# Attention stage of a fused fp32 kernel: value products of a head pair in three runs instead of four, in two PSUM banks

## Chip, cores and metric

The kernel runs on one core of a Trainium2 chip. The metric is the device time of one execution in microseconds (us): before the change 931.25 us, the median of 3 runs (930.16 to 931.75).

## What is computed

The program is an attention with pooled queries, followed by two feed-forward blocks. The change touches the attention alone:

```python
B, H, S, D = 4, 8, 1152, 64
q_pool = q.reshape(B, H, S // 2, 2, D).mean(axis=3)     # 576 queries a head
scores = (1 / sqrt(D)) * q_pool @ k.transpose(0, 1, 3, 2)
scores -= max(scores, axis=-1)
attn = exp(scores);  attn /= sum(attn, axis=-1) + 1e-9
out = attn @ v                                          # then the two blocks
```

All of it is fp32. The 32 heads are worked on as 16 pairs; after them the two blocks (matmuls with weights that the attention stage prepares on the side) take the rest of the time.

## The kernel before

**Tiles.** A pair P has nine score tiles of 128 query rows by 1152 keys: four for each head, and one (the fifth) that holds the 64 last rows of both heads. I number them 0 to 8 within the pair. Tiles alternate between two PSUM buffers of three banks each (`SC`, shown as `sc`). Two more banks, `TX` and `TY` (shown as `tx` and `ty`), serve everything else.

**One score tile** passes four stations: `scores` on TensorE (six matmuls of 384 keys, L303), `smax` on VectorE (the negated row maximum, `m`, L324), `sexp` on ScalarE (the exponential with the row sum, L336), and then a transposition, since the value product needs the keys on the partitions. There are two ways to transpose. Tiles 0 to 3 of every pair but the first are "block-turned": VectorE turns 32 by 32 blocks into the buffer `BLK` (`turn_blocks`, L356), and 16 DMAs move the blocks to their places in the tile `E` (`move_blocks`, L365, issued once a pair by SyncE). Tiles 4 to 8 are transposed by TensorE, 128 keys at a time, into PSUM (`fill`, L389: one block into the tile's own score bank, called "o", four into `ty` and four into `tx`) and copied to the tile `M` (`take`, L400: "o" and "y" by ScalarE, "x" by VectorE).

**Value products.** `E` holds the first 256 query columns of a pair (group 0), `M` the other 320 (group 1). `pv_part` (L423) multiplies one of nine key blocks of a group, for both heads: two matmuls, which the trace records as two each, so 18 matmuls and 36 records make a group. `pv_copy` (L433) copies the finished group from PSUM to the output buffer on ScalarE; `norm2` (L469, GpSimd) multiplies it with the reciprocal row sums later.

**Order.** Engines take their instructions in the order in which they are written. The loop over s, the running number of a tile (L658), writes step s like this:

```python
gaps[s]                        # pv_copy among them
take_rest()                    # "y" copy of tile s - 1
turn_blocks, sexp(s + 1), ...  # if tile s is block-turned; else fill "o", take "o", sexp(s + 1)
mids[s]
scores(s + 2)
fill(s, "y"), fill(s, "x")     # if tile s is not block-turned
smax(s + 2)
take(s, "x")                   # as above
run_pv(s)                      # value products planned for this step
sched[s]
```

So TensorE computes scores two tiles ahead, and the value products of a step stand behind the scores of that step. `shares` (L341) says in which steps the value products of pair P run, counted from the pair's first step, as (step, number of key blocks): steps 9 to 12 are steps 0 to 3 of the next pair, the four block-turned tiles, where TensorE has nothing to transpose. `pv_copy` of a group stands in the gap of the step after its last block.

**Side work.** Two tables place other work into these steps. `PREP` names the steps (with 0, 1, 2 for gap, mid and end of a step) of the preparation of the next pair; `qd` is `q_double`, a ScalarE copy of one head's query parts (L259). `PIECES` does so for the preparation of a piece of a weight: `mag` (ScalarE, L127) and `clamp` (GpSimd, L130), then three bit operations on VectorE (L134, L138, L142), then `hi`, `lo` and a store. Its load (512 KB) stands at the end of the step before the pair; SyncE issues it behind the 16 block moves and two stores, and ahead of the loads of the next keys and queries (`kn` and `qn`, 576 KB each).

Of the kernel before, what the change touches and what calls it, by code (L numbers as in the profile page):

```python
# [26 lines left out]
NP = NB * NH // 2  # L27
# [16 lines left out]
NORM = 9  # L44

PREP1 = ((1, 0, 'kh'), (1, 0, 'qs'), (1, 0, 'qm'), (1, 2, 'qo', 0), (2, 0, 'kt', 0), (2, 2, 'kl', 0, 0), (3, 0, 'kl', 0, 1), (4, 0, 'qo', 1), (4, 2, 'kt', 1), (5, 0, 'kl', 1, 0), (5, 2, 'kl', 1, 1), (5, 2, 'lk'), (5, 2, 'lq'), (5, 2, 'qd', 0), (7, 2, 'qd', 1), (20, 1, 'lv'))
PREP = ((-1, 2, 'qs'), (0, 0, 'qm'), (0, 0, 'qo', 0), (0, 2, 'qo', 1), (1, 1, 'lk'), (1, 1, 'kh'), (2, 0, 'lq'), (2, 1, 'qd', 0), (2, 2, 'kt', 0), (3, 1, 'kt', 1), (3, 1, 'qd', 1), (4, 2, 'kl', 0, 0), (5, 0, 'kl', 0, 1), (6, 0, 'kl', 1, 0), (6, 2, 'kl', 1, 1), (20, 1, 'lv'))

PIECES = {"a": ((1, 2), ((2, 2), (2, 2), (2, 2)), (9, 2), 14, 15), "x": ((1, 2), ((2, 2), (2, 2), (2, 2)), (3, 2), 5, 7)}
LATE = 5  # L50
LATE_TICK = 14
LATE_PACE = 2
# [11 lines left out]
def attn_moe_kernel(ctx: ExitStack, tc: tile.TileContext, qT, kT, vP, muk, mur, wk, wv, wr, wth, wtr, wti, wch, ident, out):  # L64
# [94 lines left out]
    def attention(first):  # L159
# [11 lines left out]
        TX = psV.tile([128, 512], F32, tag="tx", name="tx")  # L171
        TY = psV.tile([128, 512], F32, tag="ty", name="ty")
# [48 lines left out]
        kts, vns, rss, raws, qs = {}, {}, {}, {}, {}  # L221
# [58 lines left out]
        def quick(P):  # L280
            return P > 0
# [59 lines left out]
        def shares(P):  # L341

            if P == NP - 1:
                return ((8, 9),), ((8, 9),)
            return ((9, 5), (10, 4)), ((11, 5), (12, 4))

        pvs = {}

# [62 lines left out]
        def pv_part(k, x):  # L411

            P, g = k
            w = groups[g][1]
            j = (x + 3) % KT
            if x == 0:
                pvs[k] = TX if k == (NP - 1, 0) else TY
            for h in range(2):
                e = Es[k][:, h, j]
                out = pvs[k][64 * h:64 * h + 64, :w]  # L420
                if g == 0 and quick(P):
                    out = out.rearrange("p (a q) -> p a q", a=4)
                pe.matmul(out, lhsT=vns[P][:, h, j], rhs=e, start=(x == 0), stop=(x == KT - 1))  # L423
# [66 lines left out]
        for P in range(NP):  # L490
            for g, when in sorted(enumerate(shares(P)), reverse=P == NP - 1):
                j = 0
                for o, m in when:
                    n = min(P * KT + o, NT)
                    plan.setdefault(n, []).extend(((P, g), j + x) for x in range(m))
                    j += m
                assert j == KT
                if P == NP - 1:
                    at(n, pv_copy, (P, g))
                else:  # L500
                    at_gap(n + 1, pv_copy, (P, g))
            if P == NP - 1:
                for step in (norm0, norm1, norm3):
                    at(NT - 1, step, P)
                at_mid(NT, spread, P)
                at(NT, norm2, P)
            else:
                at(P * KT + NORM, norm0, P)
                at(P * KT + NORM + 1, norm1, P)
                at_mid(P * KT + NORM + 2, norm3, P)  # L510
                at(P * KT + NORM + 2, spread, P)
                at_mid(P * KT + NORM + 4, norm2, P)
            if quick(P):
                at(P * KT + 2, move_blocks, P)

        def run_pv(s):
            for k in plan.pop(s, []):
                pv_part(*k)
# [3 lines left out]
        def prep_sched(P):  # L522
            base = (P - 1) * KT
            for o, hook, name, *args in (PREP if P > 1 else PREP1):
                if P + (name[0] == "l") < NP and (P > 1 or base + o >= 3 or name != "lv"):
# [105 lines left out]
        for P in range(1, NP):  # L631
            base = P * KT
            for kind, (i, piece) in zip("x" if P == NP - 1 else "a", pieces):
                (zm, hm), bits, (z, hz), zl, zs = PIECES[kind]
                load, mag, clamp, *cuts, hi, lo, store = conv_steps(lambda i: cp.tile([128, 1536], F32R, tag="cv", name="cv"), piece, i, engines[CLO], pool)
# [601 lines left out]
```

## Time and profile before

| | us |
|---|---|
| median of 3 runs | 931.25 (930.16 to 931.75) |
| the profiled execution | 932.49 |
| its span, first to last instruction | 930.5 |
| TensorE matmuls busy | 907.8 (98%) |
| VectorE busy | 686.7 (74%) |
| GpSimd busy | 594.2 (64%) |
| ScalarE busy | 541.9 (58%) |
| idle time of the row maxima (L324) before they start, waiting for scores | 47.8 |
| idle time of the exponentials (L336), waiting for the maximum | 56.2 |

Matmuls are pipelined and their ends are modelled in the trace, so TensorE's busy share says little; start times of consecutive instructions say more. In the rows, PE is TensorE's matmuls, PEld its weight loads, DVE VectorE, ACT ScalarE, POOL GpSimd, SPq the queue of SyncE.

### The profile page before, as it was taken

Reading aid. Unit: us, or ns where it says so; the run is one execution under the profiler, and the core shown is the slowest. Engines: PE = TensorE matmul, PEld = TensorE weight load, DVE = VectorE, ACT = ScalarE, POOL = GpSimd, SP = SyncE. Lnnn points to the kernel's source line nnn. Section 1 sums busy time; section 2 is a strip of 40 time slices with the busy share of each in tenths; the row PEclk is TensorE's granted clock in tenths of the full one; section 3 lists DMA queues with packets and bytes.
Section 4 is the critical chain, followed back from the end, with each engine's and each line's share of the span. In section 5 each row is a group of like instructions: output and inputs, shape, how many; then the busy total and the mean of one; then the engine's idle time right before and its main releaser. Section 6 shows DMA issues by size and latency. Waiting matters only on the chain.

```text
span 930.5 us, 17357 instructions
## 1 busy us (share of the span) xinstructions
PE 907.8 (98%) x6292; PEld 786.4 (85%) x6292; DVE 686.7 (74%) x965; ACT 541.9 (58%) x1133; POOL 594.2 (64%) x662
## 2 busy tenths in 40 slices
PE   8999999999999999999889999998999999999998
PEld 6677777777777777768888999998999999999998
DVE  7888888888898888872699888888347663676712
ACT  8777777777777777764645565555344343443310
POOL 7877777777788777763466565666347574674631
PEclk9999999999999999999989999999899999999999
DMA  7268886777777776669323323233206200010001
GB/s 242 86 176 227 237 225 187 218 211 207 217 213 210 209 235 186 186 183 365 137 70 112 103 86 103 86 119 124 107 1 213 82 27 27 1 51 2 26 26 51
DMA packets 58773, 129.74 MB, mean 139 GB/s; under 512 B 10752, under 2 KB 29888, under 8 KB 58688
## 3 DMA queue, kind: packets, MB, share of 16 engines
q1 hardware_dynamic: 58688, 128.64, 46.4%
q8 instruction: 49, 0.80, 0.4%
q14 instruction: 36, 0.29, 0.1%
HBM read 70.46 MB, written 22.17 MB: 100 GB/s over the span
## 4 chain that ended last, share of the span: by engine, by line
PE 83%; DVE 8%; ACT 4%; issue 3%; POOL 1%; DMA 0%; SPq 0%; ACTq 0%; DVEq 0%; POOLq 0%
PE sc L303 18%; PE ty L423 16%; PE ps L1129 12%; PE ps L834 7%; PE ps L853 7%; PE ps L1148 5%; PE ps L1075 5%; PE ty L389 4%; PE tx L389 3%; PE ps L803 2%; PE sc L389 2%; DVE a L134 1%; DVE a L138 1%; ACT e L336 1%; PE ps L1033 1%
## 5 line engine op out<-in xcount | busy, mean ns | idle before, releaser
L324 DVE TENSOR_REDUCE m<-sc 128x1 f32<-128x1152 f32 x138 | 185.8, 1346 | 48.5 <-PE sc L303 47.8
L336 ACT ACTIVATE e<-sc,m 128x1152 f32<-128x1152 f32 x144 | 176.4, 1225 | 60.8 <-DVE m L324 56.2
L303 PE MATMUL sc<-kt,q 128*128 128x384 f32 (+1 forms) x864 | 192.7, 351 | 3.1 <-ACT M L400 1.7
L303 PEld LDWEIGHTS sc<-kt,q 128*128 128x128 f32 (+1 forms) x864 | 146.7, 190 | 24.4 <-issue 13.6
L834 PE MATMUL ps<-x,a 128*128 128x288 f32 x768 | 107.3, 300 | 5.8 <-DVE xt L858 4.8
L1129 PE MATMUL ps<-b,a 128*128 128x288 f32 x816 | 111.3, 296 | 0.0
L834 PEld LDWEIGHTS ps<-x,a 128*128 128x128 f32 x768 | 105.1, 193 | 6.8 <-DVE xt L858 5.5
L1129 PEld LDWEIGHTS ps<-b,a 128*128 128x128 f32 x816 | 109.4, 188 | 0.6
L853 PE MATMUL ps<-k,b 128*128 128x288 f32 x768 | 103.8, 295 | 0.1
L853 PEld LDWEIGHTS ps<-k,b 128*128 128x128 f32 x768 | 102.1, 188 | 0.6 <-ACT h L836 0.4
L202 POOL TENSOR_TENSOR kt<-kn,kh 64x576 fp32r<-64x576 f32 (+1 forms) x64 | 87.5, 1387 | 2.4
L356 DVE STREAM_TRANSPOSE blk<-e 128x1152 f32<-128x1152 f32 x60 | 81.6, 1360 | 7.4 <-ACT e L336 7.4
L423 PE MATMUL ty<-M,vn 128*64 128x320 f32 x576 | 84.4, 438 | 0.2 <-ACT M L400 0.2
L423 PEld LDWEIGHTS ty<-M,vn 128*64 128x64 f32 x576 | 38.7, 136 | 36.3 <-issue 3.8
L469 POOL TENSOR_TENSOR xt<-xt,rb 128x576 f32<-128x576 f32 x16 | 21.9, 1371 | 73.0 <-ACT xt L433 73.0
L821 POOL TENSOR_TENSOR k<-h,k 128x288 fp32r<-128x288 f32 x64 | 56.4, 897 | 18.1 <-ACT k L820 16.1
L423 PE MATMUL ty<-E,vn 128*64 128x256 f32 x540 | 64.9, 385 | 0.0
L803 PE MATMUL ps<-x,blk 128*128 128x288 f32 x384 | 56.8, 310 | 6.9 <-ACT x L782 3.5
L803 PEld LDWEIGHTS ps<-x,blk 128*128 128x128 f32 x384 | 55.1, 201 | 8.4 <-ACT x L782 4.0
L837 DVE TENSOR_TENSOR h<-h 128x288 f32<-128x288 f32 x64 | 38.5, 606 | 27.7 <-ACT h L836 27.3
L1093 ACT ACTIVATE q<-q 128x512 f32<-128x512 f32 x18 | 11.4, 632 | 79.2 <-DVE q L1090 79.2
L783 POOL TENSOR_TENSOR x<-t,x 128x288 fp32r<-128x288 f32 x52 | 44.9, 881 | 18.0 <-ACT x L782 18.0
(147 smaller groups left out, 1751.1 us busy)
## 6 DMA issues: line engine op xcount, KB each, us to landing
E<-blk SPq DMA_DIRECT2D x240, 144.0 KB
vn<-vP SPq DMA_DIRECT2D x16, 576.0 KB
kn<-kT SPq DMA_DIRECT2D x15, 576.0 KB
qn<-qT SPq DMA_DIRECT2D x15, 576.0 KB
b<-wtk SPq DMA_DIRECT2D x9, 576.0 KB
rb<-scr SPq DMA_DIRECT2D x32, 144.0 KB
out<-xt SPq DMA_DIRECT2D x32, 144.0 KB
cv<-wk SPq DMA_DIRECT2D x8, 512.0 KB
```

What stands on the lines that cost most here:

```text
L202: engines[e].tensor_tensor(out, x, hi.bitcast(F32), ALU.subtract)
L303: r = pe.matmul(sc[0:m, c, 0:384], lhsT=x, rhs=k[:, 384 * c:384 * c + 384], start=(i == 0), stop=(i == len(ops) - 1),)
L324: r = dve.tensor_reduce(m, scs[n][:, :, 0:384], axis=AX.XY, op=ALU.max, negate=True)
L336: r = act.activation(e, sc[:, :, 0:384], AF.Exp, bias=m, scale=1.0, accum_out=rss[P][:, t:t + 1])
L356: dve.transpose(out, es_[n].rearrange("p a b -> p (a b)").rearrange("p (k m i) -> p k m i", k=KT, m=4))
L389: r = pe.transpose(ps[:, 128 * j:128 * j + 128], flat[:, 128 * k:128 * k + 128], idn)
L423: pe.matmul(out, lhsT=vns[P][:, h, j], rhs=e, start=(x == 0), stop=(x == KT - 1))
L803: pe.matmul(pss[d], lhsT=WR[k][:, w, 128 * d:128 * d + 128], rhs=x[k][:, c], start=(k == 0 and n == 0), stop=(k == 3 and n == 2))
L821: pool.tensor_tensor(q[:, 1], h, q[:, 0].bitcast(F32), ALU.subtract)
L834: pe.matmul(ps, lhsT=WK[k, f // 4][:, w, 128 * (f % 4):128 * (f % 4) + 128], rhs=x[k][:, c], start=(k == 0 and n == 0), stop=(k == 3 and n ...
L853: pe.matmul(pss[d], lhsT=WV[f][:, w, 128 * d:128 * d + 128], rhs=k2[f][:, c], start=(f == 0 and n == 0), stop=(f == 7 and n == 2))
L1129: pe.matmul(pss[d], lhsT=zs[j][z][:, 128 * d:128 * d + 128], rhs=WTK[min(j, 8)][:, w, cs], start=(m == 0 and n == 0), stop=(m == 8 and n = ...
```

## The change

Four lines change. The value products of a pair run in steps 9, 10 and 11 instead of 9 to 12: six key blocks of group 0, then three of group 0 and three of group 1, then six of group 1. Group 1 accumulates in the bank `tx` instead of `ty`; the last pair keeps its banks. The second `qd` moves from the middle of step 3 to the end of step 2. `mag` and `clamp` move from the end of step 1 to the end of step 0, and the first two bit operations from step 2 to step 1; the third stays.

```diff
-PREP = (... (3, 1, 'kt', 1), (3, 1, 'qd', 1), (4, 2, 'kl', 0, 0), ...)
+PREP = (... (3, 1, 'kt', 1), (2, 2, 'qd', 1), (4, 2, 'kl', 0, 0), ...)
-PIECES = {"a": ((1, 2), ((2, 2), (2, 2), (2, 2)), (9, 2), 14, 15), ...}
+PIECES = {"a": ((0, 2), ((1, 2), (1, 2), (2, 2)), (9, 2), 14, 15), ...}
...
-            return ((9, 5), (10, 4)), ((11, 5), (12, 4))
+            return ((9, 6), (10, 3)), ((10, 3), (11, 6))
...
             if x == 0:
-                pvs[k] = TX if k == (NP - 1, 0) else TY
+                pvs[k] = TX if g == (P < NP - 1) else TY
```

The first place is TensorE in the four block-turned steps of a pair. `sc` are score buffers, `ty` and `tx` the two other banks, `E` and `M` the transposed exponentials, `vn` the values. The tile with `kh,qc` is the fifth (tile 4), whose three kinds of matmul come three times. Before:

```order
L423 MATMUL ty<-E,vn 64x256 x10
L303 MATMUL sc_121<-kt,q_0_1_125 128x384 x6
L423 MATMUL ty<-E,vn 64x256 x8
L303 MATMUL sc_120<-kh,qc_128 128x384
L303 MATMUL sc_120<-kt,q_0_0_124 64x384
L423 MATMUL ty<-M,vn 64x320 x10
L303 MATMUL sc_121<-kt,q_0_0_124 128x384 x6
L423 MATMUL ty<-M,vn 64x320 x8
L389 MATMUL sc_120<-idn,e 128x128
```

and now:

```order
L423 MATMUL ty<-E,vn 64x256 x12
L303 MATMUL sc_121<-kt,q_0_1_125 128x384 x6
L423 MATMUL ty<-E,vn 64x256 x6
L423 MATMUL tx<-M,vn 64x320 x6
L303 MATMUL sc_120<-kh,qc_128 128x384
L303 MATMUL sc_120<-kt,q_0_0_124 64x384
L423 MATMUL tx<-M,vn 64x320 x12
L303 MATMUL sc_121<-kt,q_0_0_124 128x384 x6
L389 MATMUL sc_120<-idn,e 128x128
```

The eight matmuls of group 1 that stood behind the scores of tile 5 (the last L303 row of each piece) now stand ahead of them, and the transposition of tile 4 follows those scores directly.

The second place is ScalarE in the same steps. L336 are the exponentials of tiles 2, 3 and 4, L433 the copies of the two groups, L259 the two query copies, L127 is `mag`:

```order
-L336 ACTIVATE e,rs_140<-sc_120,m 128x1152
-L127 ACTIVATE cv<-cv 128x512
+L127 ACTIVATE cv<-cv 128x512
+L336 ACTIVATE e,rs_140<-sc_120,m 128x1152
 L433 COPY xt_69<-ty 128x4x2x32
 L336 ACTIVATE e,rs_140<-sc_121,m 128x1152
 L259 CAST q_1_0_126<-q_1_0_126 64x1152
-L336 ACTIVATE e,rs_140<-sc_120,m 128x1152
 L259 CAST q_1_1_127<-q_1_1_127 64x2x576
-L433 COPY xt_69<-ty 128x320
+L433 COPY xt_69<-tx 128x320
+L336 ACTIVATE e,rs_140<-sc_120,m 128x1152
```

`mag` goes ahead of the exponential of tile 2, and the exponential of tile 4 goes behind the second query copy and behind the copy of group 1.

The third place is VectorE. L356 are the block turns of tiles 2 and 3, L324 the row maximum of tile 4 and, in the last row, of tile 5; L134, L138 and L142 are the bit operations:

```order
 L448 STREAM_TRANSPOSE rt<-r_141 128x32
-L356 STREAM_TRANSPOSE blk<-e 128x9x4x32 x2
-L324 TENSOR_REDUCE m<-sc_121 128x1
-L134 TENSOR_SCALAR cv<-cv 128x512
-L138 SCALAR_TENSOR_TENSOR cv<-cv 128x512
+L134 TENSOR_SCALAR cv<-cv 128x512
+L138 SCALAR_TENSOR_TENSOR cv<-cv 128x512
+L356 STREAM_TRANSPOSE blk<-e 128x9x4x32 x2
+L324 TENSOR_REDUCE m<-sc_121 128x1
 L142 SCALAR_TENSOR_TENSOR cv<-cv 128x512
 L324 TENSOR_REDUCE m<-sc_120 128x1
```

Two bit operations go ahead of the two turns and of the maximum of tile 4. On GpSimd `clamp` goes ahead of the cast of the next pair's keys (L199, `kh`); SyncE's order is the same.

## Rows read from the trace of the kernel before

**Rows 1.** Part 4 of the profile's page: the chain that ended last, shares of the span.

```profile
PE 83%; DVE 8%; ACT 4%; issue 3%; POOL 1%; DMA 0%; SPq 0%; ACTq 0%; DVEq 0%; POOLq 0%
```

**Rows 2.** Timeline, TensorE, steps 2 to 4 of one pair: start, length, instruction, count.

```profile
222.25 2.91 PE L423 MATMUL ty<-M,vn 128*64 128x320 f32 x20
225.09 1.34 PE L303 MATMUL sc<-kt,q 128*128 128x384 f32 x6
226.36 2.37 PE L423 MATMUL ty<-M,vn 128*64 128x320 f32 x16
228.67 0.33 PE L389 MATMUL sc<-idn,e 128*128 128x128 f32 x1
228.75 1.29 PE L303 MATMUL sc<-kt,q 128*128 128x384 f32 x6
229.88 0.60 PE L389 MATMUL ty<-idn,e 128*128 128x128 f32 x4
```

**Rows 3.** Timeline, VectorE, block turn of tile 3, maxima of tiles 4, 5, 6, [idle before].

```profile
222.20 1.38 DVE L356 STREAM_TRANSPOSE blk<-e 128x1152 f32<-128x1152 f32 x1 [0.52 <-ACT e L336]
223.50 1.32 DVE L324 TENSOR_REDUCE m<-sc 128x1 f32<-128x1152 f32 x1
...
226.52 1.35 DVE L324 TENSOR_REDUCE m<-sc 128x1 f32<-128x1152 f32 x1
230.09 1.36 DVE L324 TENSOR_REDUCE m<-sc 128x1 f32<-128x1152 f32 x1 [2.21 <-PE sc L303]
```

**Rows 4.** Timeline, ScalarE, the same steps: exponentials of tiles 2, 5, 6, 7.

```profile
217.61 1.23 ACT L336 ACTIVATE e<-sc,m 128x1152 f32<-128x1152 f32 x1 [1.29 <-DVE m L324]
...
226.25 1.15 ACT L259 CAST q<-q 64x1152 fp32r<-64x1152 f32 x1
228.78 0.43 ACT L433 COPY xt<-ty 128x320 f32<-128x320 f32 x1 [1.38 <-PE ty L423]
229.11 0.27 ACT L400 COPY M<-sc 128x128 f32<-128x128 f32 x1
229.40 1.23 ACT L336 ACTIVATE e<-sc,m 128x1152 f32<-128x1152 f32 x1
...
231.54 1.22 ACT L336 ACTIVATE e<-sc,m 128x1152 f32<-128x1152 f32 x1
...
233.70 1.22 ACT L336 ACTIVATE e<-sc,m 128x1152 f32<-128x1152 f32 x1 [0.17 <-DVE m L324]
```

**Rows 5.** Timeline, end of that pair: exponential of the next tile 0, scores of tile 2.

```profile
238.01 1.23 ACT L336 ACTIVATE e<-sc,m 128x1152 f32<-128x1152 f32 x1 [0.17 <-DVE m L324]
...
239.47 1.29 PE L303 MATMUL sc<-kt,q 128*128 128x384 f32 x6
```

**Rows 6.** Timeline, TensorE: scores of tile 5, first and last of 15 pairs.

```profile
45.21 1.34 PE L303 MATMUL sc<-kt,q 128*128 128x384 f32 x6
...
404.67 1.34 PE L303 MATMUL sc<-kt,q 128*128 128x384 f32 x6
```

**Rows 7.** Timeline, TensorE: value products of the last pair.

```profile
418.59 5.07 PE L423 MATMUL ty<-M,vn 128*64 128x320 f32 x36 [0.24 <-ACT M L400]
423.48 4.06 PE L423 MATMUL tx<-E,vn 128*64 128x256 f32 x36
```

**Rows 8.** Stretches: busy us of PE, PEld, DVE, ACT, POOL; PEclk, DMA share, GB/s.

```profile
210.00:217.00 7.00, 6.99 (x52) 5.71 (x52) 6.61 (x8) 5.64 (x11) 6.50 (x8) 1.00 0.91 314
217.00:222.00 5.00, 5.00 (x35) 3.47 (x31) 4.65 (x6) 3.30 (x6) 4.43 (x8) 1.00 0.06 24
```

**Rows 9.** Tile view of the weight pieces (ns min/median/max, starts); GpSimd's timeline.

```profile
L127 ACT ACTIVATE cv<-cv x15: 667/676/683, 39.0 to 398.4; 128x512 f32<-128x512 f32 x15
L134 DVE TENSOR_SCALAR cv<-cv x15: 404/406/779, 44.9 to 404.3; 128x512 uint32<-128x512 uint32 x15
L138 DVE SCALAR_TENSOR_TENSOR cv<-cv x15: 691/692/694, 45.7 to 404.8; 128x512 uint32<-128x512 uint32 x15
...
42.99 2.37 POOL L199 TENSOR_SCALAR kt<-kn 64x1152 fp32r<-64x1152 f32 x2
```

More of the change, by code (lines that the diff above doesn't have):

```diff
@@ L46 @@
 PREP1 = ((1, 0, 'kh'), (1, 0, 'qs'), (1, 0, 'qm'), (1, 2, 'qo', 0), (2, 0, 'kt', 0), (2, 2, 'kl', 0, 0), (3, 0, 'kl', 0, 1), (4, 0, 'qo', 1), (4, 2, 'kt', 1), (5, 0, 'kl', 1, 0), (5, 2, 'kl', 1, 1), (5, 2, 'lk'), (5, 2, 'lq'), (5, 2, 'qd', 0), (7, 2, 'qd', 1), (20, 1, 'lv'))
-PREP = ((-1, 2, 'qs'), (0, 0, 'qm'), (0, 0, 'qo', 0), (0, 2, 'qo', 1), (1, 1, 'lk'), (1, 1, 'kh'), (2, 0, 'lq'), (2, 1, 'qd', 0), (2, 2, 'kt', 0), (3, 1, 'kt', 1), (3, 1, 'qd', 1), (4, 2, 'kl', 0, 0), (5, 0, 'kl', 0, 1), (6, 0, 'kl', 1, 0), (6, 2, 'kl', 1, 1), (20, 1, 'lv'))
-PIECES = {"a": ((1, 2), ((2, 2), (2, 2), (2, 2)), (9, 2), 14, 15), "x": ((1, 2), ((2, 2), (2, 2), (2, 2)), (3, 2), 5, 7)}
+PREP = ((-1, 2, 'qs'), (0, 0, 'qm'), (0, 0, 'qo', 0), (0, 2, 'qo', 1), (1, 1, 'lk'), (1, 1, 'kh'), (2, 0, 'lq'), (2, 1, 'qd', 0), (2, 2, 'kt', 0), (3, 1, 'kt', 1), (2, 2, 'qd', 1), (4, 2, 'kl', 0, 0), (5, 0, 'kl', 0, 1), (6, 0, 'kl', 1, 0), (6, 2, 'kl', 1, 1), (20, 1, 'lv'))
+PIECES = {"a": ((0, 2), ((1, 2), (1, 2), (2, 2)), (9, 2), 14, 15), "x": ((1, 2), ((2, 2), (2, 2), (2, 2)), (3, 2), 5, 7)}
 LATE = 5
```

## The prediction

> **What bounds the kernel now.** I began with the page's chain of work that ended last: TensorE holds 83% of it [rows 1], so a change is worth what it does to the start times of TensorE's work. The idle times of the table say which loop binds in the attention stage: row maxima wait for scores, exponentials for maxima. I then read the timelines of TensorE, VectorE and ScalarE side by side over one pair, and compared all pairs: the pattern comes 15 times, first with the scores of tile 5 at 45.21, last at 404.67 [rows 6], every 359.46 / 14 = 25.68 us. I write S(k) for the scores of tile k.
>
> A pair has two parts with different bounds. In the block-turned steps TensorE runs without a pause: value products, S(5), value products, transposition of tile 4, each starting where the one before lets go [rows 2]. VectorE is done with the maximum of tile 5 long before and then idles 2.21 us [rows 3]; ScalarE idles 1.38 us until the last product of group 1, then copies it, copies a block of tile 4 and starts the exponential of tile 5 at 229.40 [rows 4].
>
> From there on no engine is alone the bound; it is a loop over two tiles. The exponential of tile 5 must end before TensorE may write its buffer again, those scores are needed for the maximum of tile 7, and this for the exponential of tile 7, which has waited for it (0.17 us): 229.40 to 233.70, 4.30 us [rows 4]. The same loop leads on to the next pair's tile 0 at 238.01, 4.31 us later, and S of the next pair's tile 2 follows at 239.47 [rows 5]. There is no slack in this chain, so **what moves the exponential of tile 5 moves the whole pair**.
>
> **The change, part by part.**
>
> *Value products.* Ahead of S(5) stood 10 + 8 + 10 matmuls, now stand 12 + 6 + 6 + 12: eight more, 16 records of the trace, all of group 1. A run of 20 such records lasts 2.84 us until the next instruction (222.25 to 225.09) and one of 16 lasts 2.31 (226.36 to 228.67) [rows 2]: 0.53 / 4 = 0.1325 us a record, and 0.19 for a run's start. The 16 cost 16 x 0.1325 = 2.12 us. The step that holds both groups passes from one bank to the other without scores between. The nearest row is the last pair, where 36 records of 320 columns give way to the other bank after 423.48 - 418.59 = 4.89 us [rows 7]; 36 x 0.1325 = 4.77, so such a border is worth at most 0.12, and I take 0.09 for it. Bounds: nothing, and the 0.19 of a run's start. S(5) then starts at 225.09 + 2.12 + 0.09 = 227.30.
>
> From there two paths lead to the exponential of tile 5:
> - Over VectorE: from S(6) to its maximum takes 228.75 to 230.09 = 1.34 us [rows 2, 3], from there to the exponential of tile 6 takes 230.09 to 231.54 = 1.45 [rows 3, 4]. Tile 5 at the same prices: 227.30 + 1.34 + 1.45 = 230.09.
> - Over ScalarE: the copy of group 1 now stands ahead of the exponential of tile 4, which is queued behind it with everything that follows on ScalarE. The copy starts 0.11 after TensorE's next instruction, and ScalarE's next begins 0.33 later (228.67, 228.78, 229.11) [rows 2, 4]: exponential of tile 4 at 227.74. TensorE's transposition follows 1.38 after its start (1.46 from 238.01 to 239.47, less the 0.08 from 228.67 to 228.75) [rows 2, 5], at 229.12. The block's copy and the exponential of tile 5 follow 0.44 and 0.29 later (228.67, 229.11, 229.40) [rows 2, 4]: 229.85.
>
> VectorE's path ends last, at 230.09 against 229.40: **0.69 us later a pair**. The change wins a little on TensorE, which loses one run, but S(5) used to run in the shadow of the fourth run, and its maximum with it. Now the exponential waits openly for both. TensorE will stand idle between S(5) and the transposition, some 0.7 us.
>
> *Second bank.* It costs no instruction. Without it the products of group 1 would have to wait for the copy of group 0 within one step. `tx` is free by then: its last reader, VectorE's copy of tile 8 of the pair before, lies before the first block turn.
>
> *Query copy.* 1.15 us of ScalarE [rows 4] go from behind the exponential of tile 4 to a place ahead of it, where ScalarE will be waiting for the end of group 1 until 227.41 anyway. Cost nothing; without that cover, up to 1.15 us a pair on the exponential of tile 4, of which 230.09 - 229.85 = 0.24 would be free.
>
> *`mag` and `clamp`.* `mag`, 0.68 us [rows 9], goes ahead of the exponential of tile 2, which waits 1.29 us for its maximum [rows 4]: hidden. It now needs its load before 217.61 instead of after 217.61 + 1.23 [rows 4]; were the load late, so would be that exponential. Against that: by 217 all transfers of a pair are in (DMA share 0.06 afterwards), and the 7 us before move 314 GB/s, 2.2 MB [rows 8]. The pieces of keys and queries are issued behind the load, 1.15 MB, so the load should be in 1.15 MB / 314 GB/s = 3.7 us before 217. `clamp` goes ahead of a key cast that the next pair needs; nothing waits for it here.
>
> *Bit operations.* 0.41 + 0.69 = 1.10 us [rows 9] now stand ahead of the turns of tiles 2 and 3 and the maximum of tile 4. That maximum began at 223.50, after a turn that had waited 0.52 [rows 3]. S(3) comes later by four records, 0.53 us at most, so the maximum starts between 223.50 + 1.10 = 224.60 and 0.53 after that, and ends 1.32 later, near 226.2 (S(4) is done by then: the run behind it starts at 222.25 + 12 x 0.1325 + 0.09 = 223.9). ScalarE can use it at 227.74: 1.5 us of cover. The block moves start up to 1.5 us later; their blocks are needed a whole pair of steps later, and the load and stores queue behind them as before.
>
> *Sum.* 15 x 0.69 = 10.35 us. The profiled execution took 932.49 (span 930.5), so it would take 942.8; the median of the runs lies 1.24 below that execution, so I predict **941.6 us**. Per pair, the low end is the ScalarE path alone with a free border and no start cost, 0.45 - 0.09 = 0.36 (5.4 us); the high end is a border of 0.19 and 0.15 of further lateness, 0.94 (14.1 us).
>
> **A rule against the trace.** L134 takes 0.41 us in nearly all pairs and 0.78 in one, at 44.9 [rows 9]; just then GpSimd was casting keys, until 42.99 + 2.37 = 45.36. The other pairs have the cast behind them. The Trainium skill (SBUF — State Buffer, Who interferes with whom) says that a VectorE `tensor_scalar` in a two-port mode and a GpSimd instruction exclude each other for the whole instruction. By this rule, with which that row agrees, all 15 may take 0.78, as they now fall beside `kh` casts; the sum would not change, as 0.37 fits under the 1.5 of cover.
>
> **The rivals.**
>
> *A: TensorE stays the bound (faster).* Then the transposition of tile 4 follows S(5) after 229.88 - 228.75 = 1.13 [rows 2], at 228.43 instead of 228.67: 0.24 x 15 = 3.6 us, 927.7. It decides if S(5) to the exponential takes under 1.13 + 0.44 + 0.29 = 1.86 us. For it: TensorE's 83%. Against it: that way took 2.79 where it stood open [rows 2 to 4], and the exponential of tile 4 stands behind the copy. 9%.
>
> *B: the delay is absorbed (no change).* Tiles 5 to 8 would give the 0.69 back; 931 us. For it: all engines but TensorE idle a quarter or more. Against it: 4.30 and 4.31 us per two tiles, with a wait in each [rows 4, 5]. 5%.
>
> *C: VectorE becomes late too (much slower).* If both bit operations wait for a whole cast of 2.37 / 2 = 1.19 us [rows 9], the maximum of tile 4 ends near 226.2 + 2.38 = 228.6, 0.86 past the 227.74; ScalarE's path gives 229.85 + 0.86 = 230.71, 1.31 us a pair, 19.7 us in all: 951. The point from which it decides is 1.5 + 0.24 us of extra lateness. For it: the one row of 0.78. Against: L138 never took over 0.694. This is the skill's rule above carried to both operations. 6%.
>
> **How the numbers follow.** The forecast has 80%: 941.6, between 936.7 and 945.4. A, B and C have the other 20%, so the range needs nothing of them; I round it to 936.5 to 946.5. A measurement of this kernel can tell about 0.2% (1.9 us) from no change. Slower by more than that: forecast and C, 86%; within it: B, 5%; faster: A, 9%.
>
> **What would show it.** Right: 15 times S(5) some 2.2 us later against S(2) of its pair, a maximum of tile 5 that waits for its scores, an exponential of tile 5 that waits for that maximum, TensorE idle some 0.7 us ahead of the transposition of tile 4, and 26.4 us a pair; `mag` and the query copy without waits on the path. Wrong: S(5) ahead of 226.5, a pair at 25.7 us or less, or idle time of TensorE at another place (at a value product, a late `E`; at S(4), a late exponential of tile 2).

## The result and the profile after

The change is slower: 940.82 us, the median of 4 runs (940.73 to 941.87), against 931.49 for the kernel before on the same chip, 9.33 us more; the ratio over all runs is 1.0106, 95% interval 1.0088 to 1.0123 (the two medians alone give 1.0100). The forecast was 941.6. The profiled execution took 940.76 with a span of 938.9.

Part 4 of the page after, the chain that ended last, answers to [rows 1]. TensorE's share has fallen from 83% to 72%; VectorE, ScalarE and waits for transfers have come in:

```profile
PE 72%; DVE 11%; ACT 7%; issue 4%; DMA 3%; POOL 3%; SPq 0%; ACTq 0%; DVEq 0%; POOLq 0%
```

The timelines of the same pair answer to [rows 2 to 4]. Times run 4.62 us later here, as the scores of tile 2 of this pair start at 218.43 instead of 213.81. TensorE's timeline (start, length, instruction, count, idle before):

```profile
218.43 1.30 PE L303 MATMUL sc<-kt,q 128*128 128x384 f32 x6
219.66 2.81 PE L423 MATMUL ty<-E,vn 128*64 128x256 f32 x24
...
223.64 1.52 PE L423 MATMUL ty<-E,vn 128*64 128x256 f32 x12
224.99 1.79 PE L423 MATMUL tx<-M,vn 128*64 128x320 f32 x12
226.70 0.44 PE L303 MATMUL sc<-kh,qc 128*128 128x384 f32 x1
...
228.48 3.45 PE L423 MATMUL tx<-M,vn 128*64 128x320 f32 x24
231.86 1.32 PE L303 MATMUL sc<-kt,q 128*128 128x384 f32 x6
233.79 0.33 PE L389 MATMUL sc<-idn,e 128*128 128x128 f32 x1 [0.62 <-ACT e L336]
```

The third run ends at 231.86, and only then do the scores of tile 5 start. TensorE then stands idle for 0.62 us ahead of the transposition of tile 4, where it ran without a pause before.

VectorE's timeline, the row maxima of tiles 4 and 5:

```profile
229.86 1.31 DVE L324 TENSOR_REDUCE m<-sc 128x1 f32<-128x1152 f32 x1
231.10 0.67 DVE L142 SCALAR_TENSOR_TENSOR cv<-cv 128x512 uint32<-128x512 uint32 x1
233.21 1.36 DVE L324 TENSOR_REDUCE m<-sc 128x1 f32<-128x1152 f32 x1 [1.45 <-PE sc L303]
```

The maximum of tile 5 (last row) had no wait before; now it waits 1.45 us for its scores.

ScalarE's timeline, from the two query copies to the exponential of tile 7:

```profile
226.81 2.33 ACT L259 CAST q<-q 64x1152 fp32r<-64x1152 f32 x2
231.98 0.43 ACT L433 COPY xt<-tx 128x320 f32<-128x320 f32 x1 [2.83 <-PE tx L423]
232.43 1.22 ACT L336 ACTIVATE e<-sc,m 128x1152 f32<-128x1152 f32 x1
...
234.16 0.27 ACT L400 COPY M<-sc 128x128 f32<-128x128 f32 x1 [0.42 <-PE sc L389]
234.67 1.22 ACT L336 ACTIVATE e<-sc,m 128x1152 f32<-128x1152 f32 x1 [0.24 <-DVE m L324]
...
238.97 1.22 ACT L336 ACTIVATE e<-sc,m 128x1152 f32<-128x1152 f32 x1 [0.27 <-DVE m L324]
```

The exponential of tile 4 (232.43) stands behind the copy of group 1. That of tile 5 (234.67) no longer follows the block copy ahead of it, as in [rows 4]; after that copy it waits another 0.24 us for its maximum. The exponential of tile 7 follows 4.30 us later, as before. The end of the pair answers to [rows 5]:

```profile
243.27 1.22 ACT L336 ACTIVATE e<-sc,m 128x1152 f32<-128x1152 f32 x1 [0.27 <-DVE m L324]
...
244.73 1.30 PE L303 MATMUL sc<-kt,q 128*128 128x384 f32 x6
```

From the scores of tile 2 to those of the next pair the step is 244.73 - 218.43 = 26.30 us. The first and the last scores of tile 5 answer to [rows 6]; their distance is 368.48 / 14 = 26.32 us a pair against 25.68:

```profile
47.48 1.31 PE L303 MATMUL sc<-kt,q 128*128 128x384 f32 x6
...
415.96 1.31 PE L303 MATMUL sc<-kt,q 128*128 128x384 f32 x6
```

The last pair's value products start at 428.27 against 418.59 [rows 7], so the attention stage is 9.68 us longer. I use that start below to measure the stage by itself. Between the two profiled executions the span grew by 8.4 us only; the other 1.3 lie in the feed-forward blocks (last section).

### The profile page after: what moved, and what is told of

Read it like the earlier page. It is cut to its first block, busy times and chain, and to the rows that moved or that the text cites. A ratio compares the mean times of both kernels' runs of the same rounds, so it can differ in the third digit from the quotient of the medians.

```text
span 938.9 us, 17385 instructions
## 1 busy us (share of the span) xinstructions
PE 905.3 (96%) x6292; PEld 787.8 (84%) x6292; DVE 701.0 (75%) x965; ACT 544.6 (58%) x1133; POOL 596.6 (64%) x662
## 4 chain that ended last, share of the span: by engine, by line
PE 72%; DVE 11%; ACT 7%; issue 4%; DMA 3%; POOL 3%; SPq 0%; ACTq 0%; DVEq 0%; POOLq 0%
PE sc L303 15%; PE ps L1129 12%; PE tx L423 8%; PE ty L423 7%; PE ps L1148 5%; PE ps L1075 5%; PE ps L834 5%; PE ps L853 4%; PE ty L389 3%; PE tx L389 3%; ACT e L336 3%; DMA b<-wv 2%; DVE a L134 2%; PE sc L389 2%; DVE a L138 2%
## 5 line engine op out<-in xcount | busy, mean ns | idle before, releaser
L324 DVE TENSOR_REDUCE m<-sc 128x1 f32<-128x1152 f32 x138 | 186.2, 1349 | 51.0 <-PE sc L303 48.6
L303 PE MATMUL sc<-kt,q 128*128 128x384 f32 (+1 forms) x864 | 192.4, 351 | 4.5 <-ACT M L400 1.7
L336 ACT ACTIVATE e<-sc,m 128x1152 f32<-128x1152 f32 x144 | 176.2, 1224 | 24.6 <-DVE m L324 23.4
L303 PEld LDWEIGHTS sc<-kt,q 128*128 128x128 f32 (+1 forms) x864 | 146.1, 189 | 24.6 <-issue 15.1
L356 DVE STREAM_TRANSPOSE blk<-e 128x1152 f32<-128x1152 f32 x60 | 80.3, 1356 | 0.1
L423 PE MATMUL tx<-M,vn 128*64 128x320 f32 x540 | 78.5, 435 | 0.0
L423 PEld LDWEIGHTS tx<-M,vn 128*64 128x64 f32 x540 | 37.5, 137 | 32.2 <-issue 3.7
```

The source lines that it names most:

```text
L303: r = pe.matmul(sc[0:m, c, 0:384], lhsT=x, rhs=k[:, 384 * c:384 * c + 384], start=(i == 0), stop=(i == len(ops) - 1),)
L324: r = dve.tensor_reduce(m, scs[n][:, :, 0:384], axis=AX.XY, op=ALU.max, negate=True)
L336: r = act.activation(e, sc[:, :, 0:384], AF.Exp, bias=m, scale=1.0, accum_out=rss[P][:, t:t + 1])
L356: dve.transpose(out, es_[n].rearrange("p a b -> p (a b)").rearrange("p (k m i) -> p k m i", k=KT, m=4))
```

## The experiments

I held three theories against each other (the rivals here are numbered, and are not the A, B and C of the prediction). Mine: the scores of tile 5, and then their row maximum, lie open behind the third run. Rival 1: the moved side work makes an engine late. Rival 2: what costs is the exponential of tile 4, queued behind the copy of group 1. "Pair" is the median distance between the starts of group 0's first runs in consecutive pairs; "stage" is the start of the last pair's value products.

| run | median us | ratio to before, 95% | pair us | stage us |
|---|---|---|---|---|
| before (profiled once) | 931.49 to 931.53 | 1 | 25.66 | 418.59 |
| the change | 940.82 | 1.0106 (1.0088 to 1.0123) | 26.30 | 428.27 |
| e1, value products alone | 945.13 | 1.0145 (1.0132 to 1.0159) | 26.61 | 432.75 |
| e2, side work alone | 930.63 | 0.9994 (0.9985 to 1.0002) | 25.59 | 418.00 |
| e3, third run behind the scores | 926.71 | 0.9947 (0.9932 to 0.9963) | 25.18 | 414.25 |
| e4, copy behind the exponential | 939.84 | 1.0094 (1.0081 to 1.0107) | 26.23 | 427.27 |
| e5, two blocks behind the scores | 929.28 | 0.9975 (0.9965 to 0.9986) | 25.52 | 416.71 |
| e6, one block behind the scores | 932.34 | 1.0012 (1.0003 to 1.0021) | 25.72 | 419.94 |
| e7, as e3, side work as before | 924.88 | 0.9927 (0.9914 to 0.9939) | 25.23 | 412.55 |
| e8, query copy back | 946.09 | 1.0155 (1.0141 to 1.0169) | 26.60 | 432.40 |

**e1 and e2: the two halves of the change.** The first has the new `shares` and banks with the old tables:

```diff
 PREP, PIECES: as before
-            return ((9, 5), (10, 4)), ((11, 5), (12, 4))
+            return ((9, 6), (10, 3)), ((10, 3), (11, 6))
-                pvs[k] = TX if k == (NP - 1, 0) else TY
+                pvs[k] = TX if g == (P < NP - 1) else TY
```

> Three runs and two banks alone, with the tables of side work as before. Theory (the scores and the maximum of tile 5 stand open behind the third run): like the change, 940.8 us, 26.30 us a pair, last pair's value products at 428.3 us in the trace (418.6 before). Rival 1 (the moved bit steps, mag, clamp or query copy make an engine late): the time comes back to about 931.5. Rival 2 (the exponential of tile 4, queued behind the copy of group 1, is what costs): like the change.

The second has the new tables alone:

```diff
-... (3, 1, 'qd', 1) ...   {"a": ((1, 2), ((2, 2), (2, 2), (2, 2)), ...
+... (2, 2, 'qd', 1) ...   {"a": ((0, 2), ((1, 2), (1, 2), (2, 2)), ...
```

> The side work moved as in the change, value products in four runs and one bank as before. Theory: 931.5 us as before, 25.66 us a pair, last pair's value products at 418.6. Rival 1: 935 to 941. Rival 2: 931.5.

The side work by itself costs nothing (0.9994), and the value products alone bring the whole penalty, so rival 1 falls as the cause. But e1 missed what each theory expected: it is slower than the change by 4.3 us. So with the value products as in the change, the side work in its new places saves time. ScalarE's timeline of e1, from the copy of group 1 to the exponential of tile 5, shows where:

```profile
234.24 0.43 ACT L433 COPY xt<-tx 128x320 f32<-128x320 f32 x1 [4.01 <-PE tx L423]
234.56 1.23 ACT L336 ACTIVATE e<-sc,m 128x1152 f32<-128x1152 f32 x1
...
235.91 1.16 ACT L259 CAST q<-q 64x1152 fp32r<-64x1152 f32 x1
236.97 0.25 ACT L400 COPY M<-sc 128x128 f32<-128x128 f32 x1
237.24 1.22 ACT L336 ACTIVATE e<-sc,m 128x1152 f32<-128x1152 f32 x1
```

The second query copy (235.91) stands between the exponentials of tiles 4 and 5 and holds the block copy back, and the exponential of tile 5 follows that copy without a wait. In [rows 4] the same copy lay in a wait.

**e8: the query copy alone.** To see whether it is the query copy or the bit operations, e8 is the change with that one entry put back:

```diff
-... (2, 2, 'qd', 1) ...
+... (3, 1, 'qd', 1) ...
```

> The change, with the second query copy back in the middle of the fourth step, between the exponential of tile 4 and the block copy. Theory: the copy (1.15 us) has lost its cover, since nothing waits there any more; 0.3 us a pair more than the change, as in the run with the products alone: 944 to 946, 26.6 us a pair. If the bit steps made that difference: 940.8.

It gave 946.09, a hair above the range, and 26.60 us a pair: the query copy is the whole of that difference, 0.30 us a pair.

**e3: the third run behind the scores.** The change with one number changed:

```diff
-            return ((9, 6), (10, 3)), ((10, 3), (11, 6))
+            return ((9, 6), (10, 3)), ((10, 3), (12, 6))
```

> The change, with its third run (six blocks of group 1) one step later, behind the scores of tile 5: still three runs, two banks and the moved side work. Theory: the penalty goes and one run's start is won, 0.1 to 0.25 us a pair against before: 927.5 to 930, last pair's value products at 415 to 417. Rival 1: 935 to 941, as the side work is as in the change. Rival 2: like the theory, as the copy moves back too.

926.71: not only does the penalty go, the three runs are now faster than the four of before, by 0.8 us more than the range I had given. The second bank and the step that holds both groups are still in this run, so neither is what costs. Rival 2 says the same of this run, and e4 tells the two apart.

**e4: the copy behind the exponential.** The change with the copy of group 1 one place later:

```diff
-                    at_gap(n + 1, pv_copy, (P, g))
+                    (at_mid if g else at_gap)(n + 1, pv_copy, (P, g))
```

> The change, with the copy of group 1 one place later on ScalarE, behind the exponential of tile 4. Theory: the exponential of tile 4 starts over 1 us sooner and TensorE's idle time ahead of the transposition of tile 4 goes, but the exponential of tile 5 still waits for its maximum: 940.8 us within 1.5, 26.3 us a pair. Rival 2 (the queue behind the copy is what costs): 0.65 us a pair back, 931 to 933. Rival 1: no change, 940.8.

939.84 us, 26.23 us a pair: 0.07 of the 0.64 came back. ScalarE's timeline of e4, the exponential of tile 4, the copies, the exponentials of tiles 5 and 7:

```profile
230.75 1.22 ACT L336 ACTIVATE e<-sc,m 128x1152 f32<-128x1152 f32 x1 [2.11 <-DVE m L324]
...
231.96 0.42 ACT L433 COPY xt<-tx 128x320 f32<-128x320 f32 x1
232.82 0.27 ACT L400 COPY M<-sc 128x128 f32<-128x128 f32 x1 [0.44 <-PE sc L389]
234.16 1.22 ACT L336 ACTIVATE e<-sc,m 128x1152 f32<-128x1152 f32 x1 [1.08 <-DVE m L324]
...
238.40 1.22 ACT L336 ACTIVATE e<-sc,m 128x1152 f32<-128x1152 f32 x1 [0.20 <-DVE m L324]
```

and TensorE's, the scores of tile 2 and the transposition of tile 5:

```profile
217.92 1.30 PE L303 MATMUL sc<-kt,q 128*128 128x384 f32 x6
...
235.53 0.33 PE L389 MATMUL sc<-idn,e 128*128 128x128 f32 x1 [0.82 <-ACT e L336]
```

The exponential of tile 4 has moved ahead of the copy and is done early. That of tile 5 gained nothing by it: it now waits 1.08 us for its maximum instead of 0.24, and in the pair shown TensorE's idle time has moved from the transposition of tile 4 to that of tile 5. Counted from the scores of tile 2 it starts as late as in the change: 234.16 - 217.92 = 16.24 us, and 234.67 - 218.43 = 16.24. The 0.07 lies behind it, where the exponential of tile 7 follows after 4.24 us instead of 4.30. Rival 2 falls.

**e5 and e6: how many blocks may stand ahead of the scores.** The change with two blocks, and with one, behind the scores of tile 5:

```diff
-            return ((9, 6), (10, 3)), ((10, 3), (11, 6))
+            return ((9, 6), (10, 3)), ((10, 3), (11, 4), (12, 2))   # e5
+            return ((9, 6), (10, 3)), ((10, 3), (11, 5), (12, 1))   # e6
```

> The change, with two of the nine blocks of group 1 (four matmuls) back in the fourth step, behind the scores of tile 5. Theory: a threshold. The scores of tile 5 start 13.43 - 8 x 0.1325 = 12.37 us after those of tile 2, plus 2.81 over VectorE is 15.18; TensorE's way is 12.37 + 1.27 + 1.25 + 0.73 = 15.62 and ends last, against 15.59 before and 16.24 in the change. So no penalty: 931 to 933, 25.6 to 25.8 us a pair. A cost in proportion to the blocks moved ahead would leave half of it, 936.

> As the run before, with one block (two matmuls) behind the scores of tile 5. Theory: 12.90 + 2.81 = 15.71 over VectorE, 15.62 on TensorE: both nearly equal, 0.1 us a pair above before, 932 to 934. In proportion: three quarters of the penalty, 938.5.

With 32, 34 and 36 matmuls ahead of the scores of tile 5 a pair takes 25.52, 25.72 and 26.30 us. The first two matmuls of the last four add 0.20, the other two 0.58. ScalarE's and TensorE's timelines of e6, by start, the scores of tiles 2 and 5 and the exponential of tile 5:

```profile
214.69 1.29 PE L303 MATMUL sc<-kt,q 128*128 128x384 f32 x6
...
227.58 1.34 PE L303 MATMUL sc<-kt,q 128*128 128x384 f32 x6
...
230.41 1.23 ACT L336 ACTIVATE e<-sc,m 128x1152 f32<-128x1152 f32 x1
```

The exponential of tile 5 starts 230.41 - 214.69 = 15.72 us behind the scores of tile 2, as worked out (15.71), and 16.24 in the change: 0.52 of the 0.58, where the two matmuls take 0.53 on TensorE by [rows 2]. In e5 and e6 the copy of group 1 also stands behind the exponential of tile 4, as in e4, and the other 0.06 is what e4 showed: the exponential of tile 7 follows that of tile 5 after 4.23 us in e6. A cost in proportion would have left half and three quarters of the penalty, 25.98 and 26.14 us a pair. So there is a threshold, near where I had put it. Both pairs are shorter than I had worked out, by 0.17 and 0.06 us, and the time of e5 lies 1.7 us below the range I had given.

**e7: e3 with the side work as before.** In e3 the pairs were uneven: most took 25.14 to 25.19 us, but the first four 25.43 to 25.70, one 25.34 and one 26.25. ScalarE's timeline of that one, `mag` and the exponentials of tiles 2 to 4:

```profile
241.85 0.67 ACT L127 ACTIVATE cv<-cv 128x512 f32<-128x512 f32 x1 [2.05 <-DMA cv<-wk]
242.42 1.21 ACT L336 ACTIVATE e<-sc,m 128x1152 f32<-128x1152 f32 x1
...
251.36 1.22 ACT L336 ACTIVATE e<-sc,m 128x1152 f32<-128x1152 f32 x1 [3.50 <-DVE m L324]
```

`mag` waits 2.05 us for its load. Two bit operations stand ahead of the maximum of tile 4 and need `mag` and `clamp`, so the maximum was late, and the exponential of tile 4 with it (3.50 us of waiting). In that pair TensorE stood idle for 1.02 us ahead of the transposition of tile 4:

```profile
252.73 0.33 PE L389 MATMUL sc<-idn,e 128*128 128x128 f32 x1 [1.02 <-ACT e L336]
```

e7 is the kernel before with two lines changed:

```diff
-            return ((9, 5), (10, 4)), ((11, 5), (12, 4))
+            return ((9, 6), (10, 3)), ((10, 3), (12, 6))
-                pvs[k] = TX if k == (NP - 1, 0) else TY
+                pvs[k] = TX if g == (P < NP - 1) else TY
```

> Three runs and two banks with the third run behind the scores of tile 5, and the side work where it was before the change. Theory: the pairs that were over 25.2 us with the moved side work (late loads ahead of mag) come down to 25.2, 0.5 us a pair against before: 923 to 925.5, last pair's value products near 411.5. If mag's place has no part in those pairs: 926.7 as with the moved side work.

924.88 us; all pairs now take 25.21 to 25.24 but one of 25.49. This version beats both kernels, the one before by 0.7%. TensorE's timeline of e7, the scores of tile 2, then from the second run to the transposition of tile 4:

```profile
185.88 1.30 PE L303 MATMUL sc<-kt,q 128*128 128x384 f32 x6
...
192.44 1.78 PE L423 MATMUL tx<-M,vn 128*64 128x320 f32 x12
194.15 0.44 PE L303 MATMUL sc<-kh,qc 128*128 128x384 f32 x1
...
197.00 3.45 PE L423 MATMUL tx<-M,vn 128*64 128x320 f32 x24
200.38 0.33 PE L389 MATMUL sc<-idn,e 128*128 128x128 f32 x1
```

Between the second run and the third stand the scores of tiles 4 and 5 together, and nothing waits ahead of the transposition. Whether each of the three moved pieces of side work has a part in e3's uneven pairs was not tried one by one; the wait for the load is seen in the worst of them.

## Why the prediction was right

**The chain that moves a pair.** Right. In the trace after, the exponential of tile 5 is followed by that of tile 7 after 4.30 us, by the next tile 0 after another 4.30 and by the next scores of tile 2 after 1.46, each as before. What the exponential of tile 5 lost, the pair lost: from the scores of tile 2 it starts after 16.24 us instead of 229.40 - 213.81 = 15.59, 0.65 later, and the pair is 0.64 longer. Rival B had nothing for it. The 4.30 is not a constant, though: the way from the exponential of tile 5 to that of tile 7 takes 4.23 to 4.24 us in most pairs of e4, e6 and e7 and about 4.32 in e3 and e5, so "no slack" holds to within 0.08 us.

**Start of the scores of tile 5.** Forecast 227.30, that is 13.49 us after the scores of tile 2; measured 231.86 - 218.43 = 13.43. Of the 2.21 us of delay that makes 2.15 (it was 225.09 - 213.81 = 11.28 before); the sixteen records were priced at 2.12, which leaves 0.03 for the border between the groups instead of the 0.09 I took. The price of 0.1325 us a record held: 24 records took 231.86 - 228.48 = 3.38, and 24 x 0.1325 + 0.19 = 3.37.

**Two paths to the exponential of tile 5.** VectorE's was to end 2.79 us after those scores; it took 234.67 - 231.86 = 2.81. ScalarE's was to reach the exponential of tile 4 at 227.74 + 4.62 = 232.36 and the transposition at 229.12 + 4.62 = 233.74; they came at 232.43 and 233.79. The forecast said VectorE's path ends last; e4 shows it, since shortening the other path gave 0.07 us of 0.64.

**Sum.** 0.69 us a pair was forecast, 0.64 came (26.30 against 25.66): 0.06 less at the scores' start, the border, and 0.02 more on VectorE's path. 15 pairs gave 9.68 us in the stage instead of 10.35. The 1.24 us taken off, since the profiled execution of before was that much longer than the median, were needed: the medians differ by 9.33, near the stage's 9.68, and the profiled executions by 8.27. The profiled execution after, 940.76, lies at its median; the last section shows a stretch in which that of before was longer.

**Covers.** The query copy at no cost was right, and so was naming what it would cost without a cover: e1 and e8 give 0.30 us a pair where it has none. The load of `mag` was the weak point. The forecast had the load in before the scores of tile 2; after the change `mag` waited for its load in 6 of 15 pairs, the longest time in this one, whose scores of tile 2 start at 244.73:

```profile
248.32 0.69 ACT L127 ACTIVATE cv<-cv 128x512 f32<-128x512 f32 x1 [1.18 <-DMA cv<-wk]
```

So the load came 3.6 us behind those scores. The exponential of tile 2 was then late as well: it started right behind `mag`, 248.91 - 244.73 = 4.18 us after those scores, against 222.13 - 218.43 = 3.70 in the pair above. That still cost nothing, as the pair is no longer than the others (26.30); in e3, where a pair is shorter, the cover was gone in places.

**Rivals A and C.** A needed less than 1.86 us from the scores of tile 5 to its exponential; it took 2.81, with TensorE idle for 0.62 us ahead of the transposition. Of C, half happened. The tile view of the weight pieces answers to [rows 9] (times in ns, minimum, median, maximum):

```profile
L134 DVE TENSOR_SCALAR cv<-cv x15: 385/630/1222, 41.9 to 414.0; 128x512 uint32<-128x512 uint32 x15
L138 DVE SCALAR_TENSOR_TENSOR cv<-cv x15: 691/1510/1524, 42.3 to 414.4; 128x512 uint32<-128x512 uint32 x15
```

Beside the key casts L138 takes 1.51 us instead of 0.69, which the forecast had counted against C. In the pair above it runs from 225.87, while GpSimd casts keys until 224.41 + 2.43 = 226.84:

```profile
224.41 2.43 POOL L199 TENSOR_SCALAR kt<-kn 64x1152 fp32r<-64x1152 f32 x2
```

The two operations together lengthened by 1.94 - 1.10 = 0.84 us there (0.43 + 1.51, against 0.41 + 0.69), and the maximum of tile 4 still ended at 231.17, 0.8 us ahead of the copy at 231.98. It was closer elsewhere. VectorE's timeline of the worst pair, the two operations and the maximum of tile 4:

```profile
278.00 1.22 DVE L134 TENSOR_SCALAR cv<-cv 128x512 uint32<-128x512 uint32 x1
279.25 1.52 DVE L138 SCALAR_TENSOR_TENSOR cv<-cv 128x512 uint32<-128x512 uint32 x1
...
283.25 1.31 DVE L324 TENSOR_REDUCE m<-sc 128x1 f32<-128x1152 f32 x1
```

Here they lengthened by 2.74 - 1.10 = 1.64 us, close to the 1.74 from which C decides. The maximum ended at 284.56, only 0.47 us ahead of the exponential of tile 4 (285.03), and the pair took 26.29 us like the others. So both operations did lengthen, as C had it, by up to 0.83 us each instead of 1.19, and the cover just held.

The forecast had the rule of the Trainium skill (SBUF — State Buffer, Who interferes with whom) for L134 alone. L134 took over 0.6 us in nine pairs and 0.39 to 0.47 in six, so the rule has the direction; 0.78 was neither the usual price nor the highest, and in the pair above it took 0.43 with a cast recorded beside it, so these rows do not settle whether one always keeps the other out for the whole instruction. For L138 the same section of the Trainium skill says that a VectorE instruction with two SBUF inputs contends with a GpSimd instruction that reads SBUF. The trace agrees: L138 has two such inputs, and it took 1.51 or 1.52 us in the 13 pairs where a key cast ran beside it, and 0.69 in the two where none did.

## What to carry to other kernels

Before work is moved ahead in an engine's order, look at what stands behind it and who waits for that: one fewer run was worth time here only with the scores ahead of it, and cost time with the scores behind it. The same blocks in the same three runs take 1.06% more than before (the change) or 0.53% less (e3), by one place in the order. Work put into a wait is free only as long as that wait stays, so after a change of the main chain every such cover has to be read again.

## What was not expected of the hardware

**Scores next to scores.** In e7 a pair is 25.66 - 25.23 = 0.43 us shorter than before, where I had counted 0.1 to 0.25 for one run fewer. TensorE reaches the transposition of tile 4 at 200.38 - 185.88 = 14.50 us behind the scores of tile 2, against 228.67 - 213.81 = 14.86 before: 0.36 us. Part of it is in the two sets of scores that stand side by side in e7. They take 197.00 - 194.15 = 2.85 us there. Between value products they took 228.48 - 226.70 = 1.78 in the change for tile 4 and 1.27 for tile 5 [rows 2], 3.05 together. So side by side they take 0.20 us less than apart; the other 0.16 is left for one run of value products fewer. The last 0.07 of the pair lies in the shorter way from the exponential of tile 5 to that of tile 7, 4.23 us. What in the engine makes a border between scores and value products that dear was not tried.

**The clock after an idle stretch.** In the feed-forward blocks TensorE has one wait of 3.3 us for VectorE's products (L858) in both kernels. The stretch of 36 matmuls behind that wait took 7.59 us in the profiled execution before and 6.41 in that of the change, with the same work. The rows of the stretches (busy us of PE, PEld, DVE, ACT, POOL; granted clock, DMA share, GB/s), before:

```profile
651.24:658.83 7.59, 7.59 (x36) 7.59 (x37) 1.95 (x5) 1.46 (x4) 1.98 (x3) 0.60 0.87 332
```

and after:

```profile
660.82:667.23 6.41, 6.41 (x37) 6.41 (x38) 1.95 (x5) 1.47 (x4) 1.96 (x3) 0.73 0.97 375
```

The granted clock was 0.60 in one and 0.73 in the other, a mix of the levels of 1.2 and 2.4 GHz, so the lower level lasted longer in the execution before. These 1.2 us are most of the 1.3 that the span gained outside the attention stage, in a part that the change does not touch. In the ten traces of this case the stretch took 4.90 us (e2, granted clock 1.00) to 7.59 (before), behind a wait of 3.2 to 3.4 us each time. Each kernel was profiled once, so it stays open whether the kernel or the single execution makes the difference; that the medians differ by 9.33 us, nearer to the stage's 9.68, speaks for the execution.
